# Attention in steps of two units: evacuations ahead of the minima, statistics on VectorE, copies of q and of the bits as transfers

## The chip, the cores and the metric

The kernel runs on one core of one Trainium2 chip. The metric is the device time of one execution in microseconds (us); a time stated for the kernel is the median of several runs.

## What is computed

Three layers follow each other, all in float32: attention within hash buckets, and two layers of an MLP with gates ("moe").

```python
B, H, S, D = 2, 8, 768, 64                  # q, k, v
q_bits = einsum('bhsd,dk->bhsk', q, proj) > 0    # 6 bits per position; k_bits alike
mask   = bucket(q_bits)[..., :, None] == bucket(k_bits)[..., None, :]
scores = where(mask, 0.125 * q @ k.T, -1e9)
attn   = exp(scores - scores.max(-1));  attn /= attn.sum(-1) + 1e-9
x      = (attn @ v)  as 1536 tokens x 512
x = gate1(x @ w_in1) @ w_out1 / 6           # gate1(h) = h * clip(h + 3, 0, 6)
out = mish(x @ w_in2) @ w_out2              # 512 -> 2048 -> 512, both layers
```

## The kernel before

Products that must keep float32 accuracy are split into a high part in a rounded format that TensorE multiplies fast (float32r) and the low rest. So a product is two or three matmuls.

**The attention stage** (span from about 9 to 272 us) goes through 8 pairs of heads. A pair has 12 *units* (`unit`, line 535): two halves of the queries, two heads, three blocks of 128 queries. `NU` is 96. For unit n, `attention_step(n)` (line 635) issues, one unit per step:

- `emit_S(n)`: the scores of 128 queries against 768 keys, four float32r matmuls into the double bank s0 or s1 (by n's parity). 12 rows of bits under k and q add a large value where the buckets differ, so the smallest value of a row is the best score, negated.
- `emit_pv` for unit n-11: four pieces of matmul, 64 columns wide for each of two heads, that multiply transposed probabilities by v. Six of them make a group of 384 queries of two heads; the group's bank is `pv` or `m`.
- `emit_T(n-5)`: six transposes on TensorE into banks t0 (first half of the keys) and t1.
- `emit_min(n)` on VectorE, `emit_exp(n)` on ScalarE (with the sum of the row), and the evacuations `emit_tevac` of the transposes: t0 by ScalarE, t1 by VectorE.
- After every third unit `emit_stats` (GpSimd, three small operations) and, in the next step, `emit_recip` (VectorE's reciprocal and a small product on GpSimd), then three norms `emit_norm` on GpSimd, which scale the probabilities.
- `emit_pv_hi` (ScalarE) and `emit_pv_lo` (VectorE) split a finished group into x's high and low parts.

The engines work their queues in the order of issue, and this order is written out by hand in `attention_step`. The next pair is prepared between the units by `prep(p, s)` (line 458), s counting units: the bits matmuls `prep_z` (called z here; 8 pieces into bank m) with VectorE's comparison, the high and low parts of q and k (`q_hi` on GpSimd, `q_lo` on VectorE, `k_hi` on ScalarE, `k_lo` on GpSimd), a second copy of q's high part (`q_dup`, ScalarE) and the bits into the operands (`bits_out`: k's on GpSimd, q's on ScalarE). Loads of q, k, v and weights are transfers that SP's queue issues in order, each after the tile that it overwrites has been read.

**Weights** are split by bit operations in some ten steps (`w_a_act` to `w_c_hi`, lines 123 to 173) on VectorE and ScalarE; a *weight unit* is 128 rows of one matrix. Four units are finished during attention (`w_parts`, placed by `AHEAD`), and for five more (`w_low`) the work on the low words is done at its end.

**The drain** (lines 698 to 708): after the last S, twelve more steps finish transposes and pv; between them stand the first blocks of the MLP, h0 to h4 and y0 to y2 (`emit_h`, `emit_y`), their gates (`g_parts`) and one weight unit per step (`w_push`). From line 715 on, `moe_step` runs the rest: per block twelve matmuls of h and twelve of y.

Of the kernel before, what the change touches and what calls it, by code (L numbers as in the profile page):

```python
# [8 lines left out]
F32 = mybir.dt.float32  # L9
# [11 lines left out]
def bucket_attention_two_moe_kernel(  # L21
# [51 lines left out]
    three = const.tile([128, 1], F32, name="three")  # L73

# [45 lines left out]

    w_low = range(2 * PRE, 2 * PRE + 5)

# [53 lines left out]
    def w_slot(ua, ub, uc, hooks=()):  # L176
        hooks = list(hooks)

        def hook():
            if hooks:  # L180
                hooks.pop(0)()

        hook()
        if uc is not None:
            w_c_lo(uc)
        if ua is not None and ua not in w_low:
            w_a_shift(ua)
        if ub is not None and ub not in w_low:
            w_b_act(ub)
        hook()  # L190
        hook()
        if ub is not None:
            w_b_shift(ub)
            w_b_or(ub)
        if ua is not None:
            w_a_act(ua)
            if ua not in w_low:
                w_a_or(ua)
# [40 lines left out]
    with tc.manual_schedule():  # L239
# [131 lines left out]
        with ExitStack() as actx:  # L371
# [29 lines left out]
            def prep_z(p, hf, heads=(0, 1), tag="m"):  # L401
                if hf == 0 and 0 in heads:
                    bit_t[p] = qk_p.tile([128, S], F32, tag="bits", name="bits")
# [13 lines left out]
            def bits_out(p, nm, h, eng=G):  # L417
                g = zsrc.index((nm, h))
                src = bit_t[p][32 * g:32 * g + NZ]
# [17 lines left out]
            def q_dup(p, h):  # L437
                A.copy(QA[p % 2][h][lo_], QB[p % 2][h][lo_].bitcast(F32))

            def k_hi(p, h):  # L440
                A.copy(KA[p % 2][h], raw_t[p, "k", h])
# [14 lines left out]
            DELAY = (0, 1, 0, 0) + (0,) * (NPAIR - 4)  # L456

            def prep(p, s):
                if s == 1:
                    prep_z(p, 0)()  # L460
                    q_hi(p, 0, G)
                    q_hi(p, 1, G)
                elif s == 2:
                    prep_z(p, 1)()
                    k_hi(p, 0)
                elif s == 3:
                    q_lo(p, 0)
                    q_dup(p, 0)
                elif s == 4:
                    q_lo(p, 1)  # L470
                    k_lo(p, 0)
                    bits_out(p, "k", 0)
                elif s == 5:
                    load(p + 1, ("k", 0), ("q", 0), ("q", 1))
                elif s == 6:
                    k_hi(p, 1)
                elif s == 7:
                    k_lo(p, 1)
                    bits_out(p, "k", 1)
                    q_dup(p, 1)  # L480
                elif s == 8:
                    bits_out(p, "q", 0)
                    load(p + 1, ("k", 1))
                elif s == 9:
                    bits_out(p, "q", 1)
# [9 lines left out]
            V.memset(three, 3.0)  # L495
            for g, o in enumerate((0, 32 + NB, 64, 96 + NB)):
# [3 lines left out]
            k_hi(0, 0)  # L500
# [8 lines left out]
            k_hi(0, 1)  # L509
# [21 lines left out]
            L = 5  # L531
# [20 lines left out]

            def emit_min(n):
                if n % 3 == 0:
                    st_t[n // 3] = sm_p.tile([128, 5, 3], F32, tag="st", name="st")
                V.tensor_reduce(out=st_t[n // 3][:, 0, n % 3:n % 3 + 1], in_=s_t[n][:, :, :HALF],  # L556
                                op=ALU.min, axis=AX.XY)

            def emit_exp(n):
                pt = p_p.tile([128, 2, HALF], F32, tag="p", name="p")  # L560
                st = st_t[n // 3]
                A.activation(out=pt, in_=s_t.pop(n)[:, :, :HALF], func=AF.Exp, scale=-1.0,  # L562
                             bias=st[:, 0, n % 3:n % 3 + 1], accum_out=st[:, 1, n % 3:n % 3 + 1])
# [3 lines left out]
            def emit_stats(b):  # L567
                st = st_t[b]
                G.tensor_scalar(out=st[:, 4], in0=st[:, 0], scalar1=BIG / 2, scalar2=1.0 / S,
                                op0=ALU.is_ge, op1=ALU.mult)  # L570
                G.tensor_scalar(out=st[:, 3], in0=st[:, 0], scalar1=BIG / 2, scalar2=1.0,
                                op0=ALU.is_lt, op1=ALU.mult)
                G.tensor_scalar(out=st[:, 2], in0=st[:, 1], scalar1=1e-9, scalar2=1.0,
                                op0=ALU.add, op1=ALU.mult)

            def emit_recip(b):
                st = st_t[b]
                V.reciprocal(out=st[:, 2], in_=st[:, 2])
                G.tensor_tensor(out=st[:, 3], in0=st[:, 3], in1=st[:, 2], op=ALU.mult)  # L579

            def emit_norm(n):
                st = st_t[n // 3]
                i = n % 3
# [51 lines left out]
            def attention_step(n):  # L635
# [3 lines left out]
                if live:  # L639
                    emit_S(n)  # L640
                if 0 <= m < NU:
                    emit_pv(m // 6, m % 6)
                if 0 <= u < NU:
                    emit_T(u)
                done = m - 1
                if done >= 0 and done % 6 == 5 and done < NU:
                    emit_pv_hi(done // 6)
                if live:
                    emit_min(n)
                if 0 <= u < NU:  # L650
                    emit_tevac(u, 0, acp)
                    emit_tevac(u, 1, vcp if n < NU else acp)
                if n % 3 == 0 and 0 < n <= NU:
                    emit_recip(n // 3 - 1)
                    for i in range(3):
                        emit_norm(n - 3 + i)
                if done >= 0 and done % 6 == 5 and done < NU:
                    emit_pv_lo(done // 6)
                    if done // 6 % 2 == 1 and done // 12 + 2 < NPAIR:
                        load_v(done // 12 + 2)  # L660
                if live:
                    emit_exp(n)
                if n % 3 == 2 and n < NU:
                    emit_stats(n // 3)
                if live:
                    for p in (n // 12, n // 12 + 1):
                        if 0 < p < NPAIR:
                            prep(p, n - 12 * (p - 1) - DELAY[p])

            AT = 3  # L670
            AHEAD = (4, 6, 7, 8, 9, 10, 22, 24)
            for n in range(NU):
                attention_step(n)
                if n < 2:
                    late_prep(n)
# [3 lines left out]
                for u in range(2 * PRE):  # L679
                    at = n - 12 * u - 12  # L680
                    if at in AHEAD:
                        w_parts(u)[AHEAD.index(at)]()
                for u in w_low:
                    at = n - (NU - 5 * AT) - AT * (u - 2 * PRE)
                    if at == 0:
                        w_a_shift(u)
                    elif at == 1:
                        w_a_or(u)
                    elif at == 2:
                        w_b_act(u)  # L690
# [7 lines left out]
            drain = ("h0", "g0", "h1", "g1", "", "h2", "g2", "", "h3", "g3", "", "h4")  # L698
            for n in range(NU, NU + L + 7):
                attention_step(n)  # L700
                hooks = ()
                if drain[n - NU]:
                    i = int(drain[n - NU][1])
                    if drain[n - NU][0] == "h":
                        moe_pe(i)
                    else:
                        hooks = g_parts(i)
                w_push(2 * PRE + n - NU, hooks)
# [48 lines left out]
```

## Time and profile before

| | us |
|---|---|
| runs shown | 802.59, 803.49, 804.08; median 803.49 |
| the profiled execution: time | 802.6 |
| the profiled execution: span from the first to the last instruction | 800.8 |
| TensorE busy | 780.3 (97% of the span) |
| VectorE busy | 501.0 (63%) |
| ScalarE busy | 446.1 (56%) |
| GpSimd busy | 194.7 (24%), all of it before about 266 us |

The page of the profile names the engines PE (TensorE), DVE (VectorE), ACT (ScalarE), POOL (GpSimd) and SP. A TensorE row is busy from the start of a matmul to its modelled end, and matmuls overlap; the distances between starts tell how fast the engine goes. TensorE's granted clock reads 1.00 of full speed in every slice of the span.

### The profile page before, as it was taken

How to read it: one execution, taken by the hardware profiler on the slowest of the kernel's cores; microseconds unless marked ns; L12 is line 12 of the kernel's file. 1: busy time of each engine (PE TensorE's matmuls, PEld its weight loads, DVE VectorE, ACT ScalarE, POOL GpSimd, SP SyncE). 2: the span in 40 equal slices, each digit the busy share in tenths (PEclk: the TensorE clock that was granted, in tenths of full speed). 3: DMA queues.
4: the chain of work that ended last, by engine and by line, in shares of the span. 5: the costliest groups of instructions: out<-in, count | busy, mean ns of one | idle time of the engine just before them, and what ended most of it. 6: DMA issues, size and time to landing. Idle time of an engine off the chain costs nothing.

```text
span 800.8 us, 10435 instructions
## 1 busy us (share of the span) xinstructions
PE 780.3 (97%) x3776; PEld 582.6 (73%) x3776; DVE 501.0 (63%) x863; ACT 446.1 (56%) x809; POOL 194.7 (24%) x276
## 2 busy tenths in 40 slices
PE   6899999999999999999999999999999999999997
PEld 2655555556566578888888888888888888888886
DVE  5667878777777799756666676848555656121211
ACT  3677778777788787545554564655444444222221
POOL 3778779788776100000000000000000000000000
PEclk9999999999999999999999999999999999999999
DMA  4502122122000243122112121122112110010001
GB/s 124 204 22 79 40 67 79 53 81 78 28 21 1 87 151 131 53 79 72 61 53 79 49 83 53 56 76 79 53 53 80 61 45 1 1 52 1 28 26 53
DMA packets 16068, 49.96 MB, mean 62 GB/s; under 512 B 2192, under 2 KB 2192, under 8 KB 16016
## 3 DMA queue, kind: packets, MB, share of 16 engines
q1 hardware_dynamic: 16016, 49.29, 19.1%
q8 instruction: 30, 0.49, 0.3%
q14 instruction: 22, 0.18, 0.1%
HBM read 46.14 MB, written 3.15 MB: 62 GB/s over the span
## 4 chain that ended last, share of the span: by engine, by line
PE 84%; POOL 9%; DVE 3%; issue 1%; ACT 1%; DMA 1%; SPq 0%; DVEq 0%; POOLq 0%; ACTq 0%
PE s L312 33%; PE t L261 16%; PE pv L261 8%; PE m L261 7%; PE s L549 6%; PE t L598 5%; POOL p L584 4%; PE pv L611 3%; POOL kb L444 2%; PE m L611 2%; PE m L408 2%; POOL kb L421 1%; POOL st L579 1%; DVE st L556 1%; ACT p L562 0%
## 5 line engine op out<-in xcount | busy, mean ns | idle before, releaser
L293 DVE TENSOR_TENSOR gl<-gr,gh 128x512 fp32r<-128x512 f32 x96 | 66.2, 690 | 118.1 <-PE s L312 111.7
L598 PEld LDWEIGHTS t<-ident,p 128*128 128x128 f32 x576 | 62.0, 142 | 63.2 <-POOL p L584 25.9
L562 ACT ACTIVATE p<-s,st 128x768 f32<-128x768 f32 x96 | 86.8, 904 | 32.4 <-DVE st L556 31.8
L584 POOL TENSOR_SCALAR p<-p,st 128x768 f32<-128x768 f32 x96 | 103.9, 1094 | 3.5
L289 ACT CAST gh<-gr 128x512 fp32r<-128x512 f32 x96 | 59.8, 623 | 67.4 <-PE s L312 45.8
L556 DVE TENSOR_REDUCE st<-s 128x1 f32<-128x768 f32 x96 | 91.2, 950 | 8.0 <-PE s L549 6.4
L598 PE MATMUL t<-ident,p 128*128 128x128 f32 x576 | 85.4, 284 | 6.5 <-POOL p L584 5.6
L261 PE MATMUL t<-xh,wih 128*128 128x512 f32 x192 | 74.9, 390 | 0.0
L261 PE MATMUL t<-xh,wil 128*128 128x512 f32 x192 | 74.7, 389 | 0.0
L261 PE MATMUL t<-xl,wih 128*128 128x512 f32 x192 | 74.7, 389 | 0.0
L312 PE MATMUL s<-gh,woh 128*128 128x512 f32 x192 | 74.7, 389 | 0.0
L312 PE MATMUL s<-gh,wol 128*128 128x512 f32 x192 | 74.7, 389 | 0.0
L312 PE MATMUL s<-woh,gh 128*128 128x512 f32 x192 | 74.7, 389 | 0.0
L312 PE MATMUL s<-wol,gh 128*128 128x512 f32 x192 | 74.7, 389 | 0.0
L447 ACT COPY pt<-t 128x384 f32<-128x384 f32 x101 | 47.9, 480 | 34.4 <-PE t L598 33.8
L448 DVE COPY pt<-t 128x384 f32<-128x384 f32 x91 | 50.3, 552 | 22.8 <-PE t L598 22.2
L549 PE MATMUL s<-ka,qa 128*128 128x384 f32 x192 | 60.1, 395 | 0.8 <-DVE qa L434 0.5
L141 DVE SCALAR_TENSOR_TENSOR raw<-raw 128x512 uint32<-128x512 uint32 x64 | 44.3, 691 | 17.0 <-ACT raw L137 17.0
L549 PE MATMUL s<-kb,qb 76*128 76x384 f32 x192 | 51.6, 351 | 1.9 <-DVE kb L421 1.9
L312 PE MATMUL s<-woh,gl 128*128 128x512 f32 x192 | 51.8, 389 | 0.0
L312 PE MATMUL s<-gl,woh 128*128 128x512 f32 x192 | 51.3, 389 | 0.0
L611 PE MATMUL pv<-pt,vn 128*64 128x384 f32 x192 | 43.6, 512 | 0.0
(113 smaller groups left out, 1516.4 us busy)
## 6 DMA issues: line engine op xcount, KB each, us to landing
raw<-in_moe_w_in_dram SPq DMA_DIRECT2D x32, 512.0 KB, 3.3
raw<-in_moe_w_out_dram SPq DMA_DIRECT2D x32, 512.0 KB, 3.3
k<-in_k_dram SPq DMA_DIRECT2D x32, 192.0 KB, 3.3
q<-in_q_dram SPq DMA_DIRECT2D x16, 192.0 KB, 3.6
vn<-in_v_dram SPq DMA_DIRECT2D x8, 384.0 KB, 4.1
out_dram<-yp SPq DMA_DIRECT2D x12, 256.0 KB, 2.1
pz<-in_proj_dram SPq DMA_DIRECT2D x1, 1.5 KB, 2.7
```

Source lines behind the costliest of these rows:

```text
L261: P.matmul(ps, lhsT=w[:, cs], rhs=x[t][:, c, :], start=(n == 0), stop=(n == 3 * KB - 1))
L289: A.copy(new_g(i)[0], gr_t[i])
L293: V.tensor_tensor(out=gl, in0=gr_t.pop(i), in1=gh.bitcast(F32), op=ALU.subtract)
L312: P.matmul(ys[d // 2][:, d % 2, :], lhsT=w, rhs=g, start=(j == 0 and part == 0 and n == 0), stop=(j == NH - 1 and part == 1))
L447: acp = lambda o, i: A.copy(o, i)
L448: vcp = lambda o, i: V.tensor_copy(o, i)
L549: P.matmul(ps[:, hf, :HALF], lhsT=w[rr, qs], rhs=m[rr, hf * HALF:(hf + 1) * HALF], start=(w is QA[i][h]), stop=(w is QB[i][h]))
L556: V.tensor_reduce(out=st_t[n // 3][:, 0, n % 3:n % 3 + 1], in_=s_t[n][:, :, :HALF], op=ALU.min, axis=AX.XY)
L562: A.activation(out=pt, in_=s_t.pop(n)[:, :, :HALF], func=AF.Exp, scale=-1.0, bias=st[:, 0, n % 3:n % 3 + 1], accum_out=st[:, 1, n % 3:n % ...
L584: G.tensor_scalar(out=p_t[n], in0=p_t[n], scalar1=st[:, 3, i:i + 1], scalar2=st[:, 4, i:i + 1], op0=ALU.mult, op1=ALU.add)
L598: P.transpose(ps[:, i * 128:(i + 1) * 128], src[:, hf, i * 128:(i + 1) * 128], ident)
L611: P.matmul(pv_t[gi][64 * h:64 * h + 64, :HALF], lhsT=vn_t[p][:, h, j, :], rhs=pt_t[gi, h][j // 3][:, j % 3, :], start=(j == 0), stop=(j == ...
```

## The change

- A step handles two units. TensorE's order is pv, pv, T, S, T, S. `L`, the distance in units from S to T, is 6 instead of 5; pv follows T by 6 units as before.
- The evacuations of the first transposes come first in the queues of ScalarE and VectorE. Then VectorE has the statistics of the two units of the step before, the min of the first unit, the second evacuation, the min of the second; ScalarE has the second evacuation and the two exps.
- The statistics are four operations on VectorE on tiles of two units instead of four on GpSimd and one on VectorE on tiles of three.
- `q_dup` becomes a transfer from SBUF to SBUF (except in pair 0). `bits_out` is replaced by one multiplication of all bits on GpSimd (`bits_move`; `kbig` holds the factor per row) and four transfers. `k_hi` goes from ScalarE to GpSimd (except in pair 0).
- `prep` counts steps of two units. For pair 1 it is delayed by one step.
- Weight units of the attention stage are spread over the fifth and sixth steps of each pair and the last pair, ScalarE's parts after the first evacuation, VectorE's parts at the end. `w_low` goes away.
- In the drain six steps of two units stand for twelve of one; the evacuations of the second half stay on VectorE, where both were ScalarE's before.

The core of the diff; of long functions that are replaced only the new lines stand:

```diff
-    w_low = range(2 * PRE, 2 * PRE + 5)
...
     def w_parts(u):
-        return [lambda: (w_a_act(u), w_a_shift(u)), lambda: w_a_or(u), lambda: w_a_clamp(u), lambda: w_b_shift(u),
-                lambda: w_b_or(u), lambda: (w_b_exp(u), w_b_act(u)), lambda: w_c_lo(u), lambda: w_c_hi(u)]
+        return ([lambda: w_a_shift(u), lambda: w_a_act(u), lambda: w_b_act(u), None, None, lambda: w_c_hi(u)],
+                [None, lambda: w_a_or(u), lambda: (w_a_clamp(u), w_b_shift(u)), lambda: w_b_or(u),
+                 lambda: (w_b_exp(u), w_c_lo(u)), None])
...
             def q_dup(p, h):
-                A.copy(QA[p % 2][h][lo_], QB[p % 2][h][lo_].bitcast(F32))
+                if p == 0:
+                    return A.copy(QA[0][h][lo_], QB[0][h][lo_].bitcast(F32))
+                nc.sync.dma_start(out=QA[p % 2][h][lo_].bitcast(F32), in_=QB[p % 2][h][lo_].bitcast(F32))
...
+            def bits_move(p):
+                G.tensor_scalar(out=bit_t[p], in0=bit_t[p].bitcast(F32), scalar1=kbig, scalar2=1.0,
+                                op0=ALU.mult, op1=ALU.mult)
+                for g, (nm, h) in enumerate(zsrc):
+                    nc.sync.dma_start(out={"k": KX, "q": QB}[nm][p % 2][h][64:64 + NZ].bitcast(F32),
+                                      in_=bit_t[p][32 * g:32 * g + NZ].bitcast(F32))
...
             def prep(p, s):
+                s -= p == 1
+                if s in (0, 1):
+                    prep_z(p, s)()
+                if s == 0:
                     q_hi(p, 0, G)
                     q_hi(p, 1, G)
+                elif s == 1:
+                    k_hi(p, 0)
+                    k_hi(p, 1)
+                    q_dup(p, 0)
+                    q_dup(p, 1)
                 elif s == 2:
+                    bits_move(p)
+                    q_lo(p, 0)
                 elif s == 3:
                     q_lo(p, 1)
                     k_lo(p, 0)
                 elif s == 4:
+                    k_lo(p, 1)
+                    load(p + 1, ("k", 0), ("q", 0), ("q", 1))
                 elif s == 5:
+                    load(p + 1, ("k", 1))
...
             def emit_stats(b):
                 st = st_t[b]
+                V.tensor_scalar(out=st[:, 4], in0=st[:, 0], scalar1=BIG / 2, scalar2=1.0 / S,
                                 op0=ALU.is_ge, op1=ALU.mult)
+                V.tensor_scalar(out=st[:, 2], in0=st[:, 1], scalar1=1e-9, scalar2=None, op0=ALU.add)
                 V.reciprocal(out=st[:, 2], in_=st[:, 2])
+                V.scalar_tensor_tensor(out=st[:, 3], in0=st[:, 0], scalar=BIG / 2, in1=st[:, 2],
+                                       op0=ALU.is_lt, op1=ALU.mult)
...
+            def attention_step(n, w_act=(), w_dve=()):
                 u = n - L
                 m = n - (L + 6)
                 live = n < NU
+                for k in (m, m + 1):
+                    if 0 <= k < NU:
+                        emit_pv(k // 6, k % 6)
+                for k in range(2):
+                    if 0 <= u + k < NU:
+                        emit_T(u + k)
+                    if live:
+                        emit_S(n + k)
+                out_now = m >= 0 and m % 6 == 4
+                evac = 0 <= u < NU
+                if evac:
+                    emit_tevac(u, 0, acp)
+                if out_now:
+                    emit_pv_hi(m // 6)
+                for part in w_act:
+                    part()
+                if evac:
+                    emit_tevac(u, 1, vcp)
+                if 0 <= n - 2 < NU:
+                    emit_stats(n // 2 - 1)
+                    emit_norm(n - 2)
+                    emit_norm(n - 1)
                 if live:
                     emit_min(n)
+                if evac:
+                    emit_tevac(u + 1, 0, acp)
                 if live:
                     emit_exp(n)
+                if evac:
+                    emit_tevac(u + 1, 1, vcp)
+                if live:
+                    emit_min(n + 1)
+                    emit_exp(n + 1)
+                if out_now:
+                    emit_pv_lo(m // 6)
...
+            w_steps = [6 * p + j for p in range(1, NPAIR - 1) for j in (4, 5)] + [NU // 2 - 6 + j for j in range(6)]
...
+            drain = (("h0", "g0"), ("h1", "g1"), ("", ""), ("h2", "g2"), ("h3", "g3"), ("h4", ""))
```

## Rows read from the trace of the kernel before

**Rows 1.** The page's part 4: shares of the chain that ended last, by engine.
```profile
PE 84%; POOL 9%; DVE 3%; issue 1%; ACT 1%; DMA 1%; SPq 0%; DVEq 0%; POOLq 0%; ACTq 0%
```

**Rows 2.** Busy by stretch: PE, PEld, DVE, ACT, POOL, clock, DMA share, GB/s.
```profile
40.00:256.00 216.00, 211.22 (x1273) 125.95 (x1272) 167.09 (x268) 165.06 (x336) 168.28 (x237) 1.00 0.18 51
```

**Rows 3.** Timeline of TensorE, one unit without waits: start, us, engine, line, operation.
```profile
211.24 0.59 PE L549 MATMUL s<-ka,qa 128*128 128x384 f32 x2
...
212.12 0.87 PE L611 MATMUL pv<-pt,vn 128*64 128x384 f32 x4
212.92 0.88 PE L598 MATMUL t<-ident,p 128*128 128x128 f32 x6
213.55 0.60 PE L549 MATMUL s<-ka,qa 128*128 128x384 f32 x2
```

**Rows 4.** The same timeline: two S with a bits matmul between them.
```profile
205.63 0.62 PE L549 MATMUL s<-ka,qa 128*128 128x384 f32 x2
...
208.91 0.62 PE L549 MATMUL s<-ka,qa 128*128 128x384 f32 x2
```

**Rows 5.** The same timeline: the S of unit 12 and of unit 95.
```profile
43.27 0.60 PE L549 MATMUL s<-ka,qa 128*128 128x384 f32 x2
...
255.75 0.60 PE L549 MATMUL s<-ka,qa 128*128 128x384 f32 x2
```

**Rows 6.** The chain in order of time, around 70 us: start, us, what.
```profile
67.91 1.97 POOL kb L444
...
72.66 0.99 POOL p L584
```

**Rows 7.** Timeline of TensorE in the drain: three pv in a row.
```profile
280.82 2.16 PE L611 MATMUL m<-pt,vn 128*64 128x384 f32 x12
282.90 0.50 PE L261 MATMUL t<-xh,wih 128*128 128x512 f32 x1
```

**Rows 8.** Timeline of TensorE in the start-up: T between two S.
```profile
36.21 0.60 PE L549 MATMUL s<-ka,qa 128*128 128x384 f32 x2
...
37.00 0.82 PE L598 MATMUL t<-ident,p 128*128 128x128 f32 x6
37.59 0.62 PE L549 MATMUL s<-ka,qa 128*128 128x384 f32 x2
```

**Rows 9.** Timeline of VectorE, 107.9 to 109.9 us.
```profile
107.94 0.61 DVE L632 TENSOR_TENSOR xl<-m,xh 128x128 fp32r<-128x128 f32 x2
108.47 0.94 DVE L556 TENSOR_REDUCE st<-s 128x1 f32<-128x768 f32 x1
109.33 0.54 DVE L448 COPY pt<-t 128x384 f32<-128x384 f32 x1
109.80 0.16 DVE L578 RECIPROCAL st<-st 128x3 f32<-128x3 f32 x1
109.88 0.93 DVE L556 TENSOR_REDUCE st<-s 128x1 f32<-128x768 f32 x1
```

**Rows 10.** Groups by line: exp and q_lo; count, busy us, mean ns, idle before.
```profile
L562 ACT ACTIVATE p<-s,st 128x768 f32<-128x768 f32 x96 | 86.8, 904 | 32.4 <-DVE st L556 31.8
...
L434 DVE SCALAR_TENSOR_TENSOR qa<-q,qb 64x768 fp32r<-64x768 f32 x16 | 18.4, 1150 | 0.5
```

**Rows 11.** One line's instructions, a weight's low words on VectorE: ns min/median/max.
```profile
L141 DVE SCALAR_TENSOR_TENSOR raw<-raw x64: 662/689/758, 63.9 to 676.3; 128x512 uint32<-128x512 uint32 x64
```

**Rows 12.** One line's instructions, the loads of q and k (L391).
```profile
DMA to landing us min/median/max: 2.8/3.4/4.9
```

**Rows 13.** Timeline of TensorE in the drain: the starts of h1 and h4.
```profile
265.61 0.48 PE L261 MATMUL s<-xh,wih 128*128 128x512 f32 x1
...
290.02 0.50 PE L261 MATMUL pv<-xh,wih 128*128 128x512 f32 x1
```

**Rows 14.** Timeline around 104 us: three norms on GpSimd.
```profile
103.95 3.59 POOL L584 TENSOR_SCALAR p<-p,st 128x768 f32<-128x768 f32 x3
```

**Rows 15.** One line's instructions, a weight operation on VectorE: ns min/median/max.
```profile
L154 DVE TENSOR_SCALAR woh<-raw x32: 419/422/1054, 105.6 to 682.8; 128x512 uint32<-128x512 uint32 x32
```

More of the change, by code (lines that the diff above doesn't have):

```diff
@@ L73, in bucket_attention_two_moe_kernel @@
     three = const.tile([128, 1], F32, name="three")
+    kbig = const.tile([128, 1], F32, name="kbig")
     xh = [xpool.tile([128, KB, TW], F32R, name=f"xh{t}") for t in range(NT)]
@@ L185, in w_slot @@
             w_c_lo(uc)
-        if ua is not None and ua not in w_low:
+        if ua is not None:
             w_a_shift(ua)
-        if ub is not None and ub not in w_low:
+        if ub is not None:
             w_b_act(ub)
@@ L196, in w_slot @@
             w_a_act(ua)
-            if ua not in w_low:
-                w_a_or(ua)
+            w_a_or(ua)
         hook()
@@ L402, in prep_z @@
                 if hf == 0 and 0 in heads:
-                    bit_t[p] = qk_p.tile([128, S], F32, tag="bits", name="bits")
+                    bit_t[p] = qk_p.tile([128, S], F32R, tag="bits", name="bits")
                 ps = bank(tag)
@@ L495, in bucket_attention_two_moe_kernel @@
             V.memset(three, 3.0)
+            for g in range(4):
+                V.memset(kbig[32 * g:32 * g + 32], (BIG, 1.0)[g % 2])
             for g, o in enumerate((0, 32 + NB, 64, 96 + NB)):
@@ L499, in bucket_attention_two_moe_kernel @@
             V.tensor_copy(pz[:, NB:NZ], pz[:, :NB])
-            k_hi(0, 0)
+            k_hi(0, 0, A)
             k_lo(0, 0, V)
@@ L508, in bucket_attention_two_moe_kernel @@
             bits_out(0, "k", 0, V)
-            k_hi(0, 1)
+            k_hi(0, 1, A)
             bits_out(0, "q", 0)
@@ L667, in attention_step @@
                         if 0 < p < NPAIR:
[L668 to L675, printed above, removed]
+                            prep(p, n // 2 - 6 * (p - 1))
+                for part in w_dve:
+                    part()
+            w_steps = [6 * p + j for p in range(1, NPAIR - 1) for j in (4, 5)] + [NU // 2 - 6 + j for j in range(6)]
+            w_at = {}
+            for u in range(2 * PRE):
+                for on, parts in enumerate(w_parts(u)):
+                    for j, part in enumerate(parts):
+                        if part is not None:
+                            w_at.setdefault(w_steps[4 * u + j], ([], []))[on].append(part)
+            for n in range(0, NU, 2):
+                attention_step(n, *w_at.get(n // 2, ((), ())))
+                if n == 0:
+                    late_prep(0)
+                    late_prep(1)
                 if n == 2:
@@ L696, in bucket_attention_two_moe_kernel @@
                 new_wslot(more, f)
-            drain = ("h0", "g0", "h1", "g1", "", "h2", "g2", "", "h3", "g3", "", "h4")
-            for n in range(NU, NU + L + 7):
+            drain = (("h0", "g0"), ("h1", "g1"), ("", ""), ("h2", "g2"), ("h3", "g3"), ("h4", ""))
+            u = 2 * PRE
+            for n in range(NU, NU + L + 6, 2):
                 attention_step(n)
[L701 to L708, printed above, removed]
+                for part in drain[(n - NU) // 2]:
+                    hooks = ()
+                    if part[:1] == "h":
+                        moe_pe(int(part[1]))
+                    if part[:1] == "g":
+                        hooks = g_parts(int(part[1]))
+                    w_push(u, hooks)
+                    u += 1
         last_w = ctx.enter_context(tc.tile_pool(name="lastw", bufs=1, reuse_waits="tile"))
```

92 lines of the change are left out of this document (18 added, 74 removed).

## The prediction

> **What bounds the kernel now.** I read the shares of the chain that ended last first, then the busy time by stretch, then the TensorE timeline of the attention stage. The chain is 84% TensorE and 9% GpSimd [rows 1]. Between 40 and 256 us TensorE shows 211 of 216 us busy, VectorE, ScalarE and GpSimd 165 to 168 [rows 2]; busy shares don't tell what a step costs, the starts of the matmuls do. Where nothing waits, one unit takes 2.31 us: scores (S) to pv .88, pv to transposes (T) .80, T to the next S .63 [rows 3]. A unit with a bits matmul behind it (z) takes 3.28, so z costs .97 [rows 4]. From the S of unit 12 to the S of unit 95 there are 212.48 us [rows 5]. At the pace of rows 3 the 83 units between would take 191.7, and the 12 z of pairs 2 to 7 take 11.6; what is left, **9.1 us, are waits**. The chain shows who is waited for: GpSimd's norms in threes, with k's low part and k's bits in its queue around them [rows 6]. So the stage stands within 5% of TensorE's own pace in this order, and the waits that are left come from GpSimd. The layers behind the attention stage are not touched.
>
> **The change, step by step.** I name a time in a new step of two units from the start of its first T.
>
> 1. *TensorE's order.* The new step is pv pv, T S, T S. Two units in the old order cost 4.62. For the new one: three pv in a row (twelve pieces) take 2.08 to the next matmul [rows 7], so the first is .80 and each further one .64, two together 1.44. T after pv .63 [rows 3]. S to T is .79 and T after S .59, from the one place in the old start-up where a T stands between two S without a pv [rows 8]. The last S to pv .88. Sum 4.33, or .29 less per step: fewer changes to and from the half-width pv tiles. 83 units are 41.5 steps: **-12.0**. A z now goes between S and pv instead of T and S; I take the same .97, and if it differs by a tenth, the twelve make 1.2 either way.
>
> 2. *GpSimd.* A pair now gives it 12 norms at .99 [rows 6], two q_hi, k_hi twice, one multiplication of bits, k_lo twice. k_hi there is not in the trace: bounds .99 (the norm, same form and shape) and 1.97 (k_lo, two inputs [rows 6]); I take .99, the nearer. The new norms also come two steps before their T, where of the old batch of three the first was waited for at once. The stats leave GpSimd. Even with k_hi at the upper end a pair has some 24 us of GpSimd work for 28. So the waits go: **-9.1**. What is late next is ScalarE, in 3.
>
> 3. *VectorE and ScalarE.* VectorE issues per step: evacuation .47, four stats, min .86, evacuation .47, min .86 (start to start [rows 9]; the durations are .54 and .94). The stats are new there. Bounds: .1 each if they overlap as the reciprocal does with the min behind it (.08 from start to start), .2 each if each waits for the whole of the one before (.16 and a little). Three of the four depend on each other, so I take .6, with .4 and .8 as ends. Follow one step: T's second half is ready at .96, the stats run from 1.43 to 2.03, the second min ends at 4.30. ScalarE starts the second exp at 4.39 and needs 1.0 (.90 [rows 10] and an estimated .1 for the read of its sum), to 5.40. Behind it stands the next step's first evacuation: 5.88, with .08 for the signal 5.96. The transposes of the next step's second unit wait for that bank; at TensorE's own pace they would start at 4.33+1.42 = 5.75. The step then settles at 4.435 instead of 4.33 (twice the step is 5.96 plus the 2.91 that TensorE has from there to the second T after it). **+.10 x 41.5 = +4.2.** A longer or shorter stats chain moves the step by half its difference: with .4 nothing is left of this, with .8 it is 8. The stats stand ahead of both mins and of one evacuation in VectorE's queue; they wait for the exps of the step before, whose last sum is read by 1.2 of the new step, ahead of 1.43. The loop exp, stats, min, min, exp is 4.2, under the step.
>
> 4. *Third and fourth step of a pair.* VectorE has q_lo (.95 alone, 1.15 in the mean [rows 10]) in both, and pv's low part (.53 [rows 9]) in the third. It is .25 to .45 late for the next evacuation, against .2 of slack; what is over comes back through the exps: .3 per pair, six pairs, **+1.8**, ends 0 and 3.3. Bits, two per pair, lie under the z steps.
>
> 5. *Weights in the attention stage.* VectorE's parts of four units stand in the fifth and sixth steps, one or two operations like the .69 of [rows 11] in each, at most .2 over the slack: **+1.0**, ends 0 and 3.
>
> 6. *Transfers.* SP gains two q copies and four bits copies per pair, ScalarE loses six casts. The copies are needed three steps (13 us) after their issue; loads of q and k land in 2.8 to 4.9 [rows 12], so nothing waits for a copy: 0. But the load of k's second head moves to one step ahead of its z. It waits for k_lo, which GpSimd ends 1.7 into the last step; plus .1, .6 of issue and 3.4 it lands at 5.8, and z comes at 4.43+2.89 = 7.3. Slack 1.5. For pair 2, whose predecessor is delayed by a step, load and z fall into the same step: TensorE waits there, once, about **+2.6** (ends 0 and 4).
>
> 7. *Start.* The first loads stay. Units go two by two, without pv until 12; TensorE could do 1.38 each [rows 8], but VectorE's 3.26 a step plus q_lo in two steps gives some 41.9 for the S of unit 12, against 43.27 [rows 5]: **-1.4**, ends -4 and +3.
>
> 8. *Drain.* From the S of unit 95 the kernel before needs 9.86 us to h1 and 34.27 to h4 [rows 5, 13]. After the change five weight units have their low words' work here instead of ahead: five operations of .69 for VectorE and ten for ScalarE; and six evacuations of .47 move from ScalarE to VectorE. The second T of a step waits for VectorE's evacuation of the first, which is queued behind a weight unit and the gate of h0: VectorE's list of that step ends at 11.9, the evacuation at 12.4, so h1 starts at 12.8. The same once more for T 95; then TensorE catches up by the shorter runs of pv, and the weights are in time: h4 at 37.1, and 1.0 for y4's gate: **+3.8**, ends 0 and +7.
>
> Sum: -12.0 -9.1 +4.2 +1.8 +1.0 +2.6 -1.4 +3.8 = **-9.1**. The profiled execution has a span of 800.8 and a time of 802.6, so 791.7 and 793.5; the median of the runs shown lies .9 above that time. From 803.49 I forecast **794.4**.
>
> **Rivals.**
>
> *The shared port (slower).* Next to norms on GpSimd an operation of VectorE on SBUF alone took up to 1.05 where .42 is its median, and three norms 3.59 where three of .99 are 2.97 [rows 14, 15]: one waits for the other. The new stats read and write only SBUF, beside GpSimd's norms, k_hi and k_lo. If they wait .63 per step, half of it lengthens the step: .31 x 41.5 = +13, so 807.4; with a whole norm of .99, 814.9. From .44 per step on the gain is gone. Against it: GpSimd's norms wait for these very stats, so it is mostly idle when they come; only behind k_lo, in two of six steps, it runs on by .3. The Trainium skill, "SBUF — State Buffer", section "SBUF: two separate sides", says that the pair of ports VectorE and GpSimd share is an exclusive lock held for a whole instruction, not a split of bandwidth. By that rule a full norm of .99 would be paid wherever one has just begun; [rows 14, 15] agree with it in kind. Chance .13.
>
> *VectorE and ScalarE set the step.* Signals or evacuations later than I reckon by .37 in the chain of 3 make the step 4.62: +7.7, 802.1. For it: those engines are 77% busy already [rows 2]. Against: their sums per step are 3.3 and 3.0. Chance .12.
>
> *k arrives late in every pair.* At the slowest landing, 4.9, and with k_lo one norm later, z waits 1.0 in six pairs: +6, 800.4. Chance .06.
>
> *More is gained.* If the stats take .4, the +4.2 goes, and if the drain costs 1 instead of 3.8: 787.4. Chance .15.
>
> **How the numbers follow.** The forecast as worked out, give or take 5, has .54. A measurement of this kernel can tell about .2% (1.6 us) from no change. Faster: .51 of the forecast, .15 where more is gained, .04 of late k: .70. Same: .13, most of it where VectorE and ScalarE set the step. Slower: .17, the port and the upper ends of start and drain. The range reaches from where more is gained to just under the port's case: 786 to 806.
>
> **What would show it.** In the profile after: a plain step (S of an even unit to the next even one) of 4.4 to 4.5 where two units now take 4.62, 5.3 with a z; pv as eight pieces; no wait for GpSimd's norms, and waits of transposes for evacuations instead; one wait of 2 to 3 us for a load of k near 45 us; the S of unit 95 near 243; h1 some 13 us and h4 some 37 after it; VectorE's four stats at .6 together. I am wrong if a plain step stays at 4.6 or more, if transposes still wait for norms, or if the time from the S of unit 95 to h4 is not longer.

## The result, and the profile after

The changed kernel takes 809.58 us (median of 4 runs, 808.92 to 809.98) against 803.55 for the kernel before beside it: ratio 1.0076, interval 1.0058 to 1.0093. It is slower; the forecast was 794.4, and 809.58 lies above the range's end of 806. The profiled execution has a span of 807.6, 6.8 longer than before.

The page's parts 1 and 4, kernel after: the engines' busy time and the shares of the chain:

```profile
PE 771.5 (96%) x3776; PEld 587.7 (73%) x3776; DVE 533.1 (66%) x1032; ACT 416.2 (52%) x762; POOL 153.7 (19%) x155
...
PE 83%; DVE 12%; DMA 2%; issue 1%; POOL 1%; ACT 0%; SPq 0%; DVEq 0%; POOLq 0%; ACTq 0%
```

GpSimd's 9% of the chain [rows 1] are gone, as forecast. VectorE has taken the place: 3% became 12%. Where, the starts of the scores show (TensorE timeline):

| start of | S(12) | S(24) | S(95) | h4 | end |
|---|---|---|---|---|---|
| before [rows 5, 13] | 43.27 | 74.51 | 255.75 | 290.02 | 800.8 |
| after | 45.10 | 78.51 | 258.24 | 296.90 | 807.6 |

So of the 6.8 us, 1.8 come before S(12), 0.7 between S(12) and S(95) (213.14 in place of 212.48, where 11.5 less was forecast), 4.4 between S(95) and h4, and nothing behind. Below, a *gap* is the time from the S of an even unit to the next even one; a pair of heads has six. Pair 4 (units 48 to 59), from the same timelines, with the kernels of the experiments:

| gap | 1 (z) | 2 (z) | 3 | 4 | 5 | 6 | pair |
|---|---|---|---|---|---|---|---|
| before | 6.17 | 5.63 | 4.62 | 4.62 | 5.22 | 5.59 | 31.85 |
| after | 5.44 | 5.10 | 4.33 | 4.79 | 5.88 | 5.71 | 31.25 |
| e1, no k_lo | 5.39 | 5.10 | 4.32 | 4.80 | 4.59 | 4.32 | 28.52 |
| e2, k_lo on VectorE | 5.37 | 5.09 | 4.33 | 4.80 | 5.16 | 4.86 | 29.61 |
| e9, k_lo in quarters | 5.79 | 5.10 | 4.33 | 4.80 | 4.64 | 5.20 | 29.85 |
| e3, another order | 5.38 | 5.10 | 4.32 | 4.56 | 5.31 | 4.85 | 29.52 |
| e7, e3 + stats on GpSimd | 5.41 | 5.09 | 4.31 | 4.32 | 5.81 | 5.87 | 30.81 |
| e11, e5 + casts on ScalarE | 5.36 | 5.09 | 5.85 | 4.31 | 4.42 | 4.86 | 29.89 |
| e10, best order | 5.36 | 5.11 | 4.31 | 4.94 | 4.57 | 4.95 | 29.24 |

The third gap is TensorE's own pace in the new order. It answers to [rows 3]. Timeline of TensorE, after:

```profile
151.45 0.60 PE L556 MATMUL s<-ka,qa 128*128 128x384 f32 x2
...
153.70 1.51 PE L614 MATMUL m<-pt,vn 128*64 128x384 f32 x8
155.15 0.88 PE L601 MATMUL t<-ident,p 128*128 128x128 f32 x6
155.78 0.42 PE L556 MATMUL s<-ka,qa 128*128 128x384 f32 x1
```

4.33 us, with pv as one run of eight pieces. The fifth and sixth gaps lose it again. GpSimd's timeline there, and VectorE's:

```profile
159.91 1.83 POOL L456 TENSOR_TENSOR kb<-k,ka 64x768 fp32r<-64x768 f32 x1
...
165.80 1.82 POOL L456 TENSOR_TENSOR kb<-k,ka 64x768 fp32r<-64x768 f32 x1
```

```profile
159.05 0.95 DVE L564 TENSOR_REDUCE st<-s 128x1 f32<-128x768 f32 x1
160.03 2.53 DVE L432 SCALAR_TENSOR_TENSOR qa<-q,qb 64x768 fp32r<-64x768 f32 x1
162.59 0.56 DVE L460 COPY pt<-t 128x384 f32<-128x384 f32 x1
...
165.81 2.10 DVE L131 TENSOR_SCALAR woh<-woh 128x512 f32<-128x512 f32 x1
167.95 0.43 DVE L143 TENSOR_SCALAR woh<-woh 128x512 uint32<-128x512 uint32 x1
```

q_lo starts 0.12 behind GpSimd's k_lo and takes 2.53 where 0.95 is its length alone; the weights' clamp starts with the next k_lo and takes 2.10 where its median is 0.42. One q_lo in each of the pairs 1 to 7 takes 2.50 to 2.53. The evacuation stands behind each, and TensorE behind the evacuation:

```profile
163.21 0.55 PE L601 MATMUL t<-ident,p 128*128 128x128 f32 x3 [1.09 <-DVE pt L460]
```

Among the waits of TensorE's matmuls from 40 to 256 us this evacuation is named 18 times, with 13.4 us in all; no norm is named.

In the kernel before, GpSimd's k_lo stood beside other work of VectorE. Timelines of GpSimd and VectorE, before:

```profile
162.86 1.99 POOL L444 TENSOR_TENSOR kb<-k,ka 64x768 fp32r<-64x768 f32 x1
```

```profile
163.09 0.94 DVE L556 TENSOR_REDUCE st<-s 128x1 f32<-128x768 f32 x1
164.18 0.56 DVE L448 COPY pt<-t 128x384 f32<-128x384 f32 x1 [0.16 <-PE t L598]
```

Each of its 14 k_lo of pairs 1 to 7 had a min beside it, which reads PSUM and took 0.93 to 0.96 there, its usual length; none had a q_lo.

### The profile page after: what moved, and what is told of

Read it like the earlier page. It is cut to its first block, busy times and chain, and to the rows that moved or that the text cites. A ratio compares the mean times of both kernels' runs of the same rounds, so it can differ in the third digit from the quotient of the medians.

```text
span 807.6 us, 10568 instructions
## 1 busy us (share of the span) xinstructions
PE 771.5 (96%) x3776; PEld 587.7 (73%) x3776; DVE 533.1 (66%) x1032; ACT 416.2 (52%) x762; POOL 153.7 (19%) x155
## 4 chain that ended last, share of the span: by engine, by line
PE 83%; DVE 12%; DMA 2%; issue 1%; POOL 1%; ACT 0%; SPq 0%; DVEq 0%; POOLq 0%; ACTq 0%
PE s L310 32%; PE t L259 16%; PE pv L259 8%; PE m L259 7%; PE t L601 6%; PE s L556 5%; PE pv L614 4%; DVE st L564 3%; DVE qa L432 3%; DVE pt L460 2%; PE m L406 2%; PE m L614 2%; DMA qb<-bits 1%; DVE wih L131 1%; DMA q<-in_q_dram 1%
## 5 line engine op out<-in xcount | busy, mean ns | idle before, releaser
L587 POOL TENSOR_SCALAR p<-p,st 128x768 f32<-128x768 f32 x96 | 94.2, 990 | 98.3 <-PE t L601 56.0
L601 PEld LDWEIGHTS t<-ident,p 128*128 128x128 f32 x576 | 63.8, 143 | 65.5 <-issue 21.6
L601 PE MATMUL t<-ident,p 128*128 128x128 f32 x576 | 88.7, 285 | 22.5 <-DVE pt L460 15.0
L460 DVE COPY pt<-t 128x384 f32<-128x384 f32 x96 | 53.0, 552 | 24.5 <-PE t L601 23.9
L459 ACT COPY pt<-t 128x384 f32<-128x384 f32 x96 | 45.6, 475 | 34.3 <-PE t L601 34.2
L157 ACT ACTIVATE raw<-raw 128x512 f32<-128x512 uint32 x64 | 43.0, 671 | 1.2 <-DVE raw L139 1.2
```

The costliest lines, as they stand in the source:

```text
L459: acp = lambda o, i: A.copy(o, i)
L460: vcp = lambda o, i: V.tensor_copy(o, i)
L587: G.tensor_scalar(out=p_t[n], in0=p_t[n], scalar1=st[:, 3, i:i + 1], scalar2=st[:, 4, i:i + 1], op0=ALU.mult, op1=ALU.add)
L601: P.transpose(ps[:, i * 128:(i + 1) * 128], src[:, hf, i * 128:(i + 1) * 128], ident)
```

## The experiments

**My theory**: GpSimd's k_lo and VectorE's operations on SBUF hold each other up, and the change put k_lo beside q_lo and the weights. **The rival**: VectorE's list in these steps is too long in itself. Four kernels ran first, beside the kernel before at 803.13.

*e1.* From the changed kernel:

```diff
             def k_lo(p, h, eng=G):
+                if p > 1:
+                    return
```

> The changed kernel with GpSimd's subtraction that makes the low part of k's split left out for pairs 2 to 7: their scores use the low part that pairs 0 and 1 left behind. VectorE's list of work is untouched. Theory (GpSimd's k_lo, 1.83 us, stretches what VectorE does beside it: q_lo 2.53 in place of 0.95, the weights' clamp 2.02 in place of 0.42): q_lo of head 1 back to 0.95 to 1.15, the clamp to 0.42 to 0.6, the fifth and sixth step of a pair from 5.88 and 5.71 to 4.3 to 4.7, so 2.0 to 2.6 a pair in 6 pairs: 794 to 798 us. Rival (VectorE's own list is too long in these steps, whatever GpSimd does): q_lo stays above 2, the steps stay at 5.5 and more, 807 to 810 us.

Measured: 793.61 (793.32 to 796.31), ratio 0.9888 (0.9869 to 0.9907). Gaps 5 and 6 fall from 5.88 and 5.71 to 4.59 and 4.32 with VectorE's list untouched. VectorE's q_lo (its line's summary) has a median of 953 ns in place of 1139, and the clamp's longest falls from 2102 ns to 424. First after, then e1:

```profile
L432 DVE SCALAR_TENSOR_TENSOR qa<-q,qb x16: 943/1139/2533, 8.1 to 222.6; 64x768 fp32r<-64x768 f32 x16
...
L131 DVE TENSOR_SCALAR woh<-woh x32: 416/420/2102, 165.8 to 684.8; 128x512 f32<-128x512 f32 x32
```

```profile
L432 DVE SCALAR_TENSOR_TENSOR qa<-q,qb x16: 942/953/2515, 8.1 to 211.0; 64x768 fp32r<-64x768 f32 x16
...
L131 DVE TENSOR_SCALAR woh<-woh x32: 418/421/424, 157.8 to 671.4; 128x512 f32<-128x512 f32 x32
```

(The 2515 is pair 1's, whose k_lo stays.) The theory holds: k_lo beside VectorE costs 2.7 us a pair. What is left over TensorE's pace, some 1.1 a pair in gaps 1, 4 and 5, is not k_lo's; VectorE's own list is the likeliest cause, and no run takes that list alone out.

*e2.* In `prep` of the changed kernel:

```diff
-                    k_lo(p, 0)
+                    k_lo(p, 0, V)
...
-                    k_lo(p, 1)
+                    k_lo(p, 1, V)
```

> The changed kernel with the low part of k's split made on VectorE in the same steps, for pairs 1 to 7, so that GpSimd's subtraction is never beside VectorE's. VectorE gets 2 x 0.95 us a pair more work (the length of its own subtraction of this size) and loses the stretching, 1.6 at q_lo and 1.6 at the weights. Theory (the two engines hold each other up): about 1 us a pair better or as good, 800 to 808 us. Rival (VectorE's own list sets the step): its list grows by 0.95 in two steps of a pair that are already over 5.7, +1.9 a pair in 7 pairs, 818 to 824 us.

Measured: 798.16 (797.89 to 800.5), ratio 0.9943 (0.9926 to 0.996), better than either text said. VectorE has 1.9 us more work a pair, and yet the pair takes 1.64 less (31.25 to 29.61), and S(24) comes at 74.40 in place of 78.51, since pair 1's prep gains in the same way and gap 1 of pair 1, where pair 2's load is late, takes 6.31 in place of 8.73. The rival falls: 818 to 824 was its price. VectorE's list does count a little: with a k_lo of 0.95 more in each, gaps 5 and 6 are 0.57 and 0.54 longer than in e1.

*e3.* The prep of a pair in another order:

```diff
                 if s == 0:
                     q_hi(p, 0, G)
                     q_hi(p, 1, G)
+                    k_hi(p, 0)
                 elif s == 1:
-                    k_hi(p, 0)
                     k_hi(p, 1)
+                    k_lo(p, 0)
                     q_dup(p, 0)
                     q_dup(p, 1)
                 elif s == 2:
                     bits_move(p)
-                    q_lo(p, 0)
+                    k_lo(p, 1)
                 elif s == 3:
-                    q_lo(p, 1)
-                    k_lo(p, 0)
+                    q_lo(p, 0)
+                    load(p + 1, ("k", 0), ("k", 1))
                 elif s == 4:
-                    k_lo(p, 1)
-                    load(p + 1, ("k", 0), ("q", 0), ("q", 1))
+                    q_lo(p, 1)
+                    load(p + 1, ("q", 0))
                 elif s == 5:
-                    load(p + 1, ("k", 1))
+                    load(p + 1, ("q", 1))
```

> The changed kernel with the prep in another order, nothing left out: GpSimd's k_hi of head 0 a step earlier, k_lo in the second and third step of a pair, in which VectorE has neither q_lo nor weights; q_lo in the fourth and fifth step, in which GpSimd has the norms alone; the k loads in the fourth step, the q loads in the fifth and sixth. Theory (the stretching is what the change lost): q_lo 0.95, the clamp 0.42, steps four to six 4.3 to 4.7, 2 to 3 a pair in 7 pairs, and the k load of pair 2 is in time (4 us of steps near 45): 786 to 792 us. Rival (any place of the same work costs the same, since VectorE's other work, the reductions from PSUM and the evacuations, is stretched instead): 803 to 810 us, with the lost time in the second and third step.

Measured: 796.87 (795.77 to 797.78), ratio 0.9924 (0.9908 to 0.9941): the gain is there, but 5 us short of the theory. The fifth gap still takes 5.31. Timelines of GpSimd and VectorE in e3:

```profile
146.15 0.90 POOL L449 TENSOR_SCALAR bits<-bits,kbig 128x768 fp32r<-128x768 f32 x1
147.02 1.82 POOL L456 TENSOR_TENSOR kb<-k,ka 64x768 fp32r<-64x768 f32 x1
```

```profile
147.10 0.56 DVE L460 COPY pt<-t 128x384 f32<-128x384 f32 x1 [0.42 <-PE t L602]
147.58 1.29 DVE L578 TENSOR_SCALAR st<-st 128x2 f32<-128x2 f32 x1
148.78 0.16 DVE L580 TENSOR_SCALAR st<-st 128x2 f32<-128x2 f32 x1
```

k_lo, behind the bits, now starts ahead of the statistics, and the first of them, on two columns, takes 1.29 in place of 0.16. The evacuation beside the same k_lo, which reads PSUM, takes its usual 0.56. I had looked only at the large operations.

*e4.* The changed kernel with the drain's second evacuations on ScalarE:

```diff
-                    emit_tevac(u, 1, vcp)
+                    emit_tevac(u, 1, vcp if live else acp)
...
-                    emit_tevac(u + 1, 1, vcp)
+                    emit_tevac(u + 1, 1, vcp if live else acp)
```

> The changed kernel with the drain's second evacuations of each unit on ScalarE again, as in the kernel before; the rest is untouched. From the start of the last unit's scores to the h4 block the change takes 38.66 us, the kernel before 34.27. Theory (the evacuations on VectorE queue behind the weights' low words there): 2 to 4 us come back, 805.5 to 807.5 us. Rival (the drain waits for ScalarE's list, which has the low words' shifts that the change put back): the same or up to 2 us slower, 809 to 812 us.

Measured: 804.76 (803.39 to 808.49), ratio 1.0024 (1.0008 to 1.004), 0.7 under the theory's range. From S(95) to h4 the trace has 35.46 (255.61 to 291.07) in place of 38.66: 3.2 us, inside the theory's 2 to 4. First after, then e4: the transposes that wait in the drain, h1 (after) and the pv pieces behind the last wait:

```profile
269.14 0.52 PE L601 MATMUL t<-ident,p 128*128 128x128 f32 x3 [1.25 <-ACT pt L459]
270.56 0.55 PE L601 MATMUL t<-ident,p 128*128 128x128 f32 x3 [0.90 <-DVE pt L460]
270.86 0.47 PE L259 MATMUL s<-xh,wih 128*128 128x512 f32 x1
...
278.14 0.52 PE L601 MATMUL t<-ident,p 128*128 128x128 f32 x3 [2.02 <-ACT pt L459]
279.30 0.90 PE L601 MATMUL t<-ident,p 128*128 128x128 f32 x3 [0.64 <-DVE pt L460]
280.13 2.54 PE L614 MATMUL m<-pt,vn 128*64 128x384 f32 x8
```

```profile
266.50 0.84 PE L601 MATMUL t<-ident,p 128*128 128x128 f32 x6 [1.22 <-ACT pt L459]
...
274.18 0.52 PE L601 MATMUL t<-ident,p 128*128 128x128 f32 x3 [1.84 <-ACT pt L459]
...
275.37 1.51 PE L614 MATMUL m<-pt,vn 128*64 128x384 f32 x8
```

VectorE's waits of 0.90 and 0.64 are gone, ScalarE's stay. Of the 3.2 about 2.1 are there when the last pv pieces start (21.9 us behind S(95) after, 19.8 in e4); the other 1.0 is the run of eight pieces itself, 2.54 after and 1.51 in e4, where the granted clock doesn't fall (last section). The other 1.6 of the median's gain I can't place: e4's runs lie 5 us apart, and in the one that has a trace S(24) comes at 75.90, 2.6 earlier than after, though the edit touches nothing there (gap 1 of pair 1 takes 5.57 in place of 8.73).

The next four kernels ask for both gains together, for the price of the late load, for the value of the statistics on VectorE, and whether the hold-up goes by instruction (before: 803.69).

*e5*: the edits of e3 and e4.

> The order of prep of e3 and the drain's evacuations of e4 together, nothing left out. Theory (two separate losses, one in pairs 2 to 7 and one behind the last scores): e3's 796.9 less the 3.2 us that e4's trace shows between the last unit's scores and h4 (38.66 to 35.46): 793 to 794.5 us. Rival (e4's gain came from the k load of pair 2, which e3 has cured already): 796 to 797.5 us.

Measured: 794.3 (792.79 to 794.56), ratio 0.9882 (0.9865 to 0.9898). That is inside the theory's range: the two losses add up.

*e6.* The changed kernel, loads only:

```diff
                     q_lo(p, 1)
                     k_lo(p, 0)
+                    load(p + 1, ("k", 0))
                 elif s == 4:
                     k_lo(p, 1)
-                    load(p + 1, ("k", 0), ("q", 0), ("q", 1))
-                elif s == 5:
-                    load(p + 1, ("k", 1))
+                    load(p + 1, ("k", 1), ("q", 0), ("q", 1))
```

> The changed kernel with the two k loads alone issued a step earlier, so that pair 2's bits matmuls don't wait for them. Theory (the wait for k's load, with the slower clock that TensorE shows behind it, costs 3 us of the changed kernel, and it explains that e4's runs lie anywhere from 803 to 808): pairs 0 and 1 take 66.5 us in place of 69.35, 806 to 807.5 us. Rival (that place is slow because VectorE and GpSimd hold each other up in the start, at 38 to 41 us): as before, 809 to 810 us.

Measured: 812.15 (809.69 to 813.62), ratio 1.0105 (1.0085 to 1.0126). Both texts were wrong; it is slower. Pair 2's first bits matmul (timeline of TensorE) and SP's queue in e6:

```profile
51.54 0.85 PE L406 MATMUL m<-q,pz 64*32 64x384 f32 x1 [2.80 <-DMA q<-in_q_dram]
```

```profile
40.77 7.00 SPq L389 DMA_DIRECT2D k<-in_k_dram  x4
47.86 1.18 SPq L389 DMA_DIRECT2D q<-in_q_dram  x2
```

I had put k's load of head 1 ahead of the q loads. SP stands at it until k_lo has read the tile (k_lo ends at 46.64), and q, which is free long before, is issued at 47.86 in place of 41.69. So e6 shows what a load in the wrong place of the queue costs; what the late load costs in the changed kernel, and whether it explains the spread of e4's runs, it leaves open.

*e7.* e3 with `emit_stats` and `emit_recip` of the kernel before, on tiles of two units:

```diff
-                    emit_stats(n // 2 - 1)
+                    emit_recip(n // 2 - 1)
...
                     emit_exp(n + 1)
+                    emit_stats(n // 2)
```

> The kernel e3 with three of the statistics on GpSimd again, each pair of units behind its exps, and the reciprocal on VectorE as in the kernel before; the product of the two on GpSimd. VectorE's list is shorter by about 0.7 us a step. Theory (in e3 what is over a plain step is VectorE's own list: q_lo and weights on top of minima, evacuations and statistics): the fifth and sixth step of a pair fall from 5.31 and 4.85 to 4.6 and 4.4, 1 to 1.5 a pair in 6 pairs: 788 to 792 us. Rival (GpSimd's small operations and norms come late, the waits that the change removed are back): 797 to 805 us, with TensorE waiting for norms.

Measured: 807.92 (806.95 to 811.88), ratio 1.0066 (1.0044 to 1.0088): 11 slower than e3, beyond the rival's end. The timeline of GpSimd and VectorE around q_lo:

```profile
131.45 0.95 DVE L432 SCALAR_TENSOR_TENSOR qa<-q,qb 64x768 fp32r<-64x768 f32 x1
...
131.65 0.85 POOL L578 TENSOR_SCALAR st<-st 128x2 f32<-128x2 f32 x1
```

Now GpSimd is the one that waits, 0.85 for an operation of 0.23. TensorE's transposes wait 4.1 us for the statistics (5 times), 6.6 for VectorE's evacuations and 3.0 for ScalarE's between 40 and 256 us. Gap 4 reaches TensorE's pace, 0.25 less than in e3, so VectorE's shorter list is worth something; but 5 and 6 lose 1.5 together. In this order, statistics on VectorE are worth 11 us.

*e9.* k_lo as four instructions of a quarter of the columns, pairs 1 to 7.

```diff
+                for c in range(4 if p else 1):
+                    w = S // 4 if p else S
+                    cs = slice(c * w, c * w + w)
...
```

> The changed kernel with each subtraction of k's low part (pairs 1 to 7) cut into four of a quarter of the columns, in the same places: the same data, four instructions. Theory (VectorE's instruction waits until the instruction that GpSimd has begun is through): q_lo and the clamp wait for a quarter only, about 0.45 each in place of 1.6, and GpSimd's quarters wait in between: q_lo 1.1 to 1.6 in place of 2.53, the clamp 0.5 to 1.1 in place of 2.02, 1 to 2.5 a pair in 6 pairs: 795 to 803 us. Rival (the two share a bandwidth, so the whole of GpSimd's data has to go by): q_lo stays above 2.2, 808 to 811 us.

Measured: 802.08 (801.45 to 802.8), ratio 0.9982 (0.9973 to 0.9991), inside the theory's range. q_lo's summary:

```profile
L432 DVE SCALAR_TENSOR_TENSOR qa<-q,qb x16: 943/1143/1305, 8.2 to 215.7; 64x768 fp32r<-64x768 f32 x16
```

The longest q_lo falls from 2533 to 1305 ns beside the same data: 0.36 over its shortest, where a quarter of k_lo takes 0.59 (its line's median). So VectorE waits for the instruction that has begun, not for all of GpSimd's data, and the rival falls. That is also the rule of the Trainium skill, "SBUF — State Buffer", section "SBUF: two separate sides": the loser of the shared ports stands until the other's whole instruction is through. GpSimd pays: its four quarters beside q_lo take 2.98 in all (125.53) in place of 1.83 for the one.

The last two kernels (before: 803.19) take k_lo clear of the statistics too, and undo the moves off ScalarE.

*e10.* From e5:

```diff
                 elif s == 2:
                     bits_move(p)
-                    k_lo(p, 1)
+                    q_lo(p, 0)
                 elif s == 3:
-                    q_lo(p, 0)
-                    load(p + 1, ("k", 0), ("k", 1))
+                    k_lo(p, 1)
+                    load(p + 1, ("k", 0), ("q", 0), ("k", 1))
                 elif s == 4:
                     q_lo(p, 1)
-                    load(p + 1, ("q", 0))
-                elif s == 5:
                     load(p + 1, ("q", 1))
```

> e5 with its third and fourth step of prep changed: the multiplication of the bits beside q_lo of head 0 again, k_lo of head 1 alone in the fourth step, loads a step earlier. In e5's trace k_lo of head 1 (147.26 to 149.08) held one statistic for 1.30 us in place of 0.16, and the step behind it took 5.32 in place of 4.32. Theory (any operation of VectorE on SBUF waits for GpSimd's instruction that has begun): k_lo now starts 1 us earlier in its step and ends ahead of the statistics; the statistic is back to 0.16, the fifth gap 4.3 to 4.5, the fourth 4.6 to 4.8; 0.5 to 0.9 a pair in 6 pairs: 788 to 792 us. Rival (VectorE's own list is what is left in e5): no change, 793 to 795 us, with the late time in another step.

Measured: **790.63** (790.0 to 791.61), ratio 0.9847 (0.9834 to 0.9861): inside the theory's range, the fastest, and faster than both kernels. Timelines of GpSimd and VectorE:

```profile
149.99 1.82 POOL L456 TENSOR_TENSOR kb<-k,ka 64x768 fp32r<-64x768 f32 x1
```

```profile
149.13 0.95 DVE L563 TENSOR_REDUCE st<-s 128x1 f32<-128x768 f32 x1
150.94 0.56 DVE L460 COPY pt<-t 128x384 f32<-128x384 f32 x1 [0.86 <-PE t L600]
151.41 0.42 DVE L576 TENSOR_SCALAR st<-st 128x2 f32<-128x2 f32 x1
```

k_lo ends at 151.81, and the statistic still waits a quarter of a microsecond for that; in the fifth gap 4.57 is left of 5.32. But the fourth gap is 4.94, longer than expected, so a pair gains only 0.3. Of the 3.7 us between e5 and e10 the stage gives 1.5, its start 0.7, and the drain the rest: S(95) to h4 is 35.50 here and 37.05 in e5, where TensorE's granted clock falls to 0.59 and 0.56 (264 to 268 us) and stays at 1.00 in e10. Stretches of e5, then of e10, columns as in the last section:

```profile
264.00:266.00 2.00, 2.00 (x9) 1.02 (x11) 1.97 (x5) 1.74 (x4) 0.00 (x0) 0.59 0.66 240
266.00:268.00 2.00, 2.00 (x6) 0.70 (x3) 2.00 (x5) 2.00 (x5) 0.00 (x0) 0.56 0.00 0
```

```profile
264.00:268.00 4.00, 4.00 (x19) 3.28 (x18) 3.95 (x10) 4.00 (x8) 0.00 (x0) 1.00 0.45 133
```

The drains of the two kernels are issued alike and wait alike (3.9 us, four times, for ScalarE), so the drain's part is the clock's, and not shown to be the edit's: e5's fastest run, with a mean clock of 1.000, takes 792.79, and e10's two such runs 790.00 and 790.37. That leaves 2.4 to 2.8 us for the new order.

*e11.* From e5, in the first two steps of `prep` and in `q_dup`:

```diff
-                    k_hi(p, 0)
+                    k_hi(p, 0, A)
...
-                    k_hi(p, 1)
+                    k_hi(p, 1, A)
...
-                if p == 0:
-                    return A.copy(QA[0][h][lo_], QB[0][h][lo_].bitcast(F32))
-                nc.sync.dma_start(out=QA[p % 2][h][lo_].bitcast(F32), in_=QB[p % 2][h][lo_].bitcast(F32))
+                A.copy(QA[p % 2][h][lo_], QB[p % 2][h][lo_].bitcast(F32))
```

> e5 with q's second copy and k's high part on ScalarE again, as in the kernel before: per pair four casts of 0.83 us for ScalarE in the first two steps, two transfers less, and GpSimd has 1.7 less. Theory (the moves off ScalarE are needed: it has some 3.2 of a step of 4.3 to 5.1 already, and two casts behind its exps make the next evacuation 0.4 to 0.8 late): 0.5 to 1.5 a pair: 797 to 804 us. Rival (ScalarE's own slack covers them, and GpSimd's relief is worth as much): 792 to 795 us.

Measured: 796.7 (796.36 to 797.57), ratio 0.9921 (0.9907 to 0.9934), 0.3 under the theory's range. The third gap grows to 5.85 behind the casts, while the fifth, with GpSimd relieved, falls to 4.42. Pair 4 is 0.4 longer; over all, the moves off ScalarE are worth 2.4 us (796.7 less 794.3).

## Why the prediction was wrong

The mechanism that decided stood in the text as a rival, at .13 and 807.4, but at the wrong place. The terms:

1. *TensorE's order: right.* 4.31 to 4.33 in gap 3 against 4.33. A z costs .77 (5.10 less 4.33), not .97: the twelve give 2.4 more than forecast.
2. *GpSimd's waits: right.* No transpose in the stage waits for a norm. In e7, with the statistics back on GpSimd, transposes wait for GpSimd again, for the statistics (4.1 us).
3. *VectorE and ScalarE, +4.2: nothing.* A plain gap doesn't settle at 4.435: gap 3 has 4.33, and e1's gap 6, with three gaps without z ahead of it, 4.32. The chain through the evacuations was .1 too long on paper. The four statistics are .54 together, near the .6 taken, from the start of the first to the min behind the last (timeline of VectorE):

```profile
157.18 0.16 DVE L577 TENSOR_SCALAR st<-st 128x2 f32<-128x2 f32 x1
...
157.72 0.95 DVE L564 TENSOR_REDUCE st<-s 128x1 f32<-128x768 f32 x1
```

4. and 5. ***The step that failed.*** For q_lo and the weights I took their lengths alone or their mean (.95, 1.15 [rows 10], .69 [rows 11]), and so +1.8 and +1.0. From pair 2 to pair 6 a pair takes 31.24 in the mean; TensorE's pace gives 27.5 (four gaps of 4.32, two of 5.10). That is 3.8 too much in each, 18.8 in five, where these two terms had 2.8 in all. e1 shows 2.7 of the 3.8 to be k_lo's; the other 1.1, 5.4 in five, is more than the 2.8 too, and its cause stays open. The rows that I read said it: [rows 14, 15] show both engines stretched, and a mean of 1.15 for an operation that takes .95 alone is no length but a mixture [rows 10]. I used the rule for the statistics alone, where the rival was argued, and never laid k_lo beside what the diff puts next to it: `q_lo(p, 1)` and `k_lo(p, 0)` stand in one branch.
6. *Transfers.* No matmul of TensorE waits for a copy. In the chain's 2% for DMA q's bits stand twice (156.74 and 219.32), each ahead of a min that starts .47 behind the evacuation, its usual distance, so they cost nothing there. e11 shows q's copies together with k_hi's move worth 2.4, not the copies alone. The k load is late once, for pair 2, as forecast: gap 1 of pair 1 takes 8.73 where the others take 5.2 to 5.4, so 3.4 against +2.6.
7. *Start, -1.4: +1.8.* S(12) comes at 45.10, 41.9 was forecast. The same collision in pair 1's prep (k_lo at 38.58) is in it: with k_lo in quarters, S(12) comes at 43.24. The other 1.3 of the miss I didn't test; with the same start, S(12) came at 45.72 in e1's execution and at 45.67 in e4's.
8. *Drain, +3.8: 4.3.* h1 starts 12.6 behind S(95) (12.8 forecast), h4 38.7 (37.1). The queueing of VectorE's evacuations was right, and e4 gives 2.1 us of waits back. That the total fits is partly luck: the 1.0 for y4's gate did not come (nothing is lost behind h4), 1.0 of slower clock came that I had not counted, and TensorE's longest waits, 1.25 and 2.02, are for ScalarE's evacuations.

The sum: 791.7 was forecast for the span, 807.6 came. The stage from S(12) to S(95) is 12.1 longer than forecast (213.14 against 201.0), the start 3.2, the drain about .5. Terms 1 and 3 were 6.6 too dear and hide a part of what terms 4 and 5 missed, 16.0 in five pairs.

Most of the .17 for slower stood on the port. That chance was worked out from one place, where GpSimd is mostly idle, and should have been worked out over every pair of operations that the new order puts side by side.

## What to carry to other kernels

Where GpSimd works beside VectorE, write both lists of a step next to each other, and price VectorE's SBUF operations (down to those on two columns) with the rest of the GpSimd instruction that can be running; put GpSimd's long ones beside VectorE's reads from PSUM. A duration in a mean over shapes or neighbours is no price: look at its minimum, and at what ran beside its maximum. When loads are moved, go through the issuing queue for the one that must wait, and put it last.

## What the runs showed of the hardware

A short wait of TensorE can cost more than itself. Stretches of the kernel after: length, busy TensorE, weight loads, VectorE, ScalarE, GpSimd, granted clock, DMA share, GB/s.

```profile
48.00:50.00 2.00, 1.03 (x8) 0.14 (x4) 0.97 (x2) 1.66 (x4) 2.00 (x3) 1.00 0.51 163
50.00:53.00 3.00, 3.00 (x11) 0.89 (x10) 0.62 (x1) 0.05 (x1) 0.50 (x1) 0.53 0.58 131
...
276.00:280.00 4.00, 1.33 (x8) 0.81 (x6) 3.21 (x7) 3.73 (x9) 0.00 (x0) 0.86 0.33 106
280.00:283.00 3.00, 3.00 (x11) 1.12 (x11) 2.73 (x7) 1.89 (x4) 0.00 (x0) 0.62 0.09 36
```

Behind the wait of .97 for k, and again behind the waits of 2.02 and .64 in the drain, the granted clock reads .53 and .62, so most of the stretch was at the lower of its two levels (1.2 of 2.4 GHz), and the run of eight pv pieces takes 2.83 and 2.54 in place of 1.51. My +2.6 and +3.8 had no term for it; it is some 1.6 of the 3.4 at the load and 1.0 in the drain. The fall need not come: in e4's drain TensorE waits 1.22 and 1.84, and the clock reads 1.00 all the way from S(95) to h4. In e6, where TensorE is busy for .74 of 3.50 us (48.00 to 51.50), the clock reads .50 for the 5 us behind. The hold-up between VectorE and GpSimd goes both ways, too: in e7 GpSimd's .23 became .85 behind VectorE's q_lo.
